# Masking the first attention rows on TensorE, one scale of x for two chunks, and a re-priced instruction order in a fused attention + MLP kernel

## The chip, the cores and the metric

The kernel runs on one core of one Trainium2 chip. Its metric is the device time of one execution in microseconds (us); the time given for a kernel is the median of its runs.

## The reference

```python
scores = (1/sqrt(64)) * q @ k.T              # 4 batches, 12 heads, 448 rows, head size 64
scores = where(causal mask, -1e9, scores)
attn = exp(scores - max(scores)); attn = attn / (sum(attn) + 1e-9)
x = (attn @ v)  -> 1792 x 768                # heads side by side
h = x @ w_in                                 # w_in 768 x 2048
out = (h - tanh(h)) @ w_out                  # w_out 2048 x 768
```

q, k, v are float32; w_in and w_out arrive as float64.

## The kernel before, in words

TensorE (PE) multiplies float16 numbers, so most operands are split into a high and a low float16 part, and each product is three matmuls (high·high, high·low, low·high). `split` (L410) makes the parts: `scaled` writes the high one, and the low one is the source times a scale minus the high one, either one `scalar_tensor_tensor` on VectorE (DVE) or a scaling in place and a subtraction, both on GpSimd (POOL). Where the result of a matmul is split (`split_x`, L568) the low part is always DVE's.

The work has these parts. `first_rows` (L595) does the first 128 rows of each batch, two batches (a chunk of 256 rows) per call, in six steps of four heads: eight float32 matmuls into two banks of `bank_s`, `softmax_part` per head (a DVE pass that adds the mask and takes the row's extreme, then an exponential on ScalarE, ACT, in place in SBUF), `inverse`, a product with the inverse on POOL, four transposes and eight matmuls with v through the one bank `bank_x`, and `split_x` with the scale `s_v` of v's bound. `w_in_chunk` (L452) loads 16 pieces of w_in, decodes float64 to float32 (`decode`: a shift, an ACT pass into PSUM and a DVE pass), finds a scale for each of eight column blocks, and splits. `w_out_half` (L469) does the like for w_out in two halves. `mlp_g` (L553) runs the first MLP product `mlp1` (L519) for 16 blocks `f` of the hidden size: 18 matmuls into one of two `bank_m` banks, tanh on ACT, a DVE pass out of PSUM, and a split into g; `h_scale` (L504) prepares the scales, per block for the two first chunks (`by_block`). `mlp2` (L535) is 48 matmuls, an evacuation and a store. `attention` (L735) does the other 320 rows of each batch, head pair by head pair: `prep` loads and splits q, k and v; `weights_unit` and `weights_last` make the split softmax weights, which a DMA transposes; `values` multiplies with v.

The order in time is not the program's. Each instruction (or group) becomes an entry in `Work` (L26). `schedule` (L159) is a list scheduler run at build time: each engine takes its ready entry of lowest `rank`, with durations from `cost` (L118), and the order that comes out is emitted, one in-order queue per engine. `either` (L107) gives an entry several engines, and the strings of `CFG` (L826) say which: "AVGA" for tag `w_in` means blocks 0, 1, 2, 3 on ACT, DVE, POOL, ACT, and so on round. `RANK` (L827) holds the ranks of the parts: before, `c0` (first chunk's rows) -14.3, `att0` -13.3, `w_in` -12.8, `evac` (what empties `bank_m`) 4.2, `w_out` 7.5, `c0b` (second chunk's rows) 9.3; the MLP's matmuls run at 10 and above and the later attentions from 8.5 up. An entry that uses the SBUF port which DVE and POOL share is marked `shared` (L96 to L102), and the planner keeps two such entries from overlapping (L182, L202).

`load_v(0)` writes into `x_block`, where `first_rows` also puts x, so attention of batch 0 comes after `mlp1` of both first chunks.

Of the kernel before, what the change touches and what calls it, by code (L numbers as in the profile page):

```python
# [20 lines left out]
P = 128  # L21
# [4 lines left out]
class Work:  # L26
# [43 lines left out]
    def add(self, eng, method, args, kw):  # L70
# [36 lines left out]
    def either(self, tag, *ways):  # L107
# [6 lines left out]
        n = self.turn[tag] = self.turn.get(tag, -1) + 1  # L114
        way = CFG[tag]
        self.ops[-1].update(eng=way[n % len(way)], tag=(tag, n))

    def cost(self, eng, method, outs, ins):  # L118
# [18 lines left out]
        if eng == "A":  # L137
            return n * 0.833 + (51 if psum else 94) + 93 * aps + 93 * (len(outs) > 1), 0.0
        if eng == "G":
            if method == "tensor_tensor":  # L140
                return n * 1.885 + 148, 0.0
# [17 lines left out]
    def schedule(self):  # L159
# [15 lines left out]
        for _ in range(n):  # L175
# [6 lines left out]
            if e in o["shared"] and port > t:  # L182
# [19 lines left out]
            if e in o["shared"]:  # L202
                t = max(t, port)
                port = t + o["cost"]
# [14 lines left out]
            for j in users[i]:  # L219
                left[j] -= 1  # L220
                f = self.ops[j]["eng"]
                at[j] = max(at[j], end + (self.SAME if f == e else self.LAT)[f])
# [36 lines left out]
def attention_then_mlp(ctx, tc, qk, v, w_in, w_out, out):  # L259
# [52 lines left out]
    ones = buf([P, P], BF16, "ones")  # L312
    mask = buf([P, 3 * P], F32, "mask")
# [31 lines left out]
    small = buf([P, 192], F32, "small")  # L345
# [25 lines left out]
    G.affine_select(out=m, in_=m, pattern=[[-1, P]], compare_op=ALU.is_ge, fill=NEG, base=0, channel_multiplier=1)  # L371
    V.memset(mask_last, 0.0)
# [47 lines left out]
    us_in, us_out, us_in_max = cols(8), cols(2), cols(1)  # L420
# [24 lines left out]
    def w_in_chunk(j):  # L445
# [9 lines left out]
        acc, s = r_acc(), r_s1()  # L455
# [38 lines left out]

    r_ch, r_usg, r_sg, r_uo, r_mix = col_ring(2, 8), col_ring(2, 1), col_ring(2, 8), col_ring(2, 2), col_ring(2, 2)

    def new_chunk(n, at=0):
# [3 lines left out]
        c.ch, c.usg, c.sg, c.uo = r_ch(), r_usg(), r_sg(), r_uo()  # L501
# [51 lines left out]
    def mlp_g(c, g16=g16, tag="g", by_block=False):  # L553
        if not by_block:
            rank(RANK["evac"])
            h_scale(c)
        for f in range(NF):
            j = f // 2
            if by_block and f % 2 == 0:
# [28 lines left out]
    r_total, r_min = col_ring(3, 4), col_ring(3, 4)  # L588
# [6 lines left out]
    def first_rows(c, bs, blocks, xs, r0):  # L595

        qkf = [view(block, at, [NP, 2, P], F32) for block, at in blocks[:2]]
        vf = view(*blocks[2], [2, NP, 2 * D], F32)
        for i, b in enumerate(bs):
# [4 lines left out]
            rank(r0)  # L604
            S.dma_start(vf[:, i], v[b, :, :, 0])
        mv, c.us_x, s_v = cols(1), cols(1), cols(1)
        bound(mv, vf.rearrange("p a n d -> p (a n d)"))
        bound_scale(c.us_x, s_v, mv, 2, mx_c)
        x = view(x_block, xs * 4 * P * NP * 2, [NP, 2, 2 * P], F16)
        c.x = [x[:, i] for i in range(NP)]  # L610
        for i in range(2):
            for g in range(H // 4):
                total, mn = r_total(), r_min()
# [244 lines left out]
```

## Time and profile before

| | |
|---|---|
| time, median of 3 runs | 605.71 us (604.11 to 606.19) |
| profiled execution, own time | 603.75 us |
| its span (first to last instruction) | 602.0 us |
| PE busy | 559.2 us (93%) |
| DVE busy | 451.6 us (75%) |
| ACT busy | 294.8 us (49%) |
| POOL busy | 312.9 us (52%) |
| DMA, mean | 123 GB/s; 327 to 337 GB/s from 15 to 45 us |

An engine's busy time is summed over its instructions. Busy shares are means over stages that have different limits, so the stages have to be read one by one. Matmuls are pipelined: what counts on PE is the distance between them, which a run of them in the timeline gives.

### The profile page before, as it was taken

What the parts mean: (1) busy time and instruction counts of PE and PEld (TensorE: products, weight loads), DVE (VectorE), ACT (ScalarE), POOL (GpSimd) and SP (SyncE); (2) the same over time, 40 slices, a digit from 0 to 9 for tenths busy, and PEclk for the clock granted to TensorE, in tenths of its full rate; (3) what the DMA queues carried; (4) which work ended last, traced back from release to release, by engine and by line L of the source; (5) the groups of instructions that cost most, each with busy time, mean ns of one, the idle gap of its engine ahead of it and who ended that gap; (6) DMA issues with size and microseconds to landing.
All of it is one profiled execution on the core that took longest, in us unless ns stands there. A gap on an engine that the chain in (4) does not pass through costs nothing.

```text
span 602.0 us, 13635 instructions
## 1 busy us (share of the span) xinstructions
PE 559.2 (93%) x5144; PEld 375.9 (62%) x5144; DVE 451.6 (75%) x1286; ACT 294.8 (49%) x796; POOL 312.9 (52%) x389
## 2 busy tenths in 40 slices
PE   3688689999999999999999999999999999999997
PEld 3456468876555556765666666665666566776664
DVE  3889997989999999999959999921999961332000
ACT  5899899983366755553436463400644430121000
POOL 3577962883232157886528788510687820465000
PEclk9999899999999999999999999999999999999999
DMA  8995467645386974448563556640334281000100
GB/s 283 327 337 186 141 196 212 188 127 222 95 164 142 181 164 79 80 99 181 119 141 72 106 123 174 128 74 27 84 60 79 42 146 43 13 2 1 27 27 26
DMA packets 113378, 74.02 MB, mean 123 GB/s; under 512 B 89760, under 2 KB 99488, under 8 KB 112800
## 3 DMA queue, kind: packets, MB, share of 16 engines
q1 hardware_dynamic: 113312, 73.15, 48.8%
q8 instruction: 40, 0.66, 0.5%
q14 instruction: 26, 0.21, 0.1%
HBM read 45.61 MB, written 5.51 MB: 85 GB/s over the span
## 4 chain that ended last, share of the span: by engine, by line
PE 31%; DVE 31%; issue 3%; DMA 3%; POOL 3%; ACT 1%; DVEq 0%; SPq 0%; POOLq 0%; ACTq 0%
PE b_m L232 29%; DVE pn L232 6%; DVE prob L232 6%; DVE small L232 5%; DVE first L232 3%; DVE t L232 3%; DVE g L232 2%; PE b_x L232 2%; DVE v L232 2%; DVE k L232 1%; DMA e<-in_v_dram 1%; DVE x L232 1%; DMA slot<-in_qk_dram 1%; POOL g L232 1%; DMA pt<-pn 1%
## 5 line engine op out<-in xcount | busy, mean ns | idle before, releaser
L232 PE MATMUL b_m<-x,w_in 128*128 128x320 f16 (+1 forms) x1728 | 230.1, 291 | 15.3 <-DVE t L232 14.2
L232 PEld LDWEIGHTS <-w_in 128*128 128x128 f16 x1728 | 167.5, 98 | 72.1 <-issue 22.9
L232 PE MATMUL b_m<-slot,g 128*128 128x384 f16 x1152 | 192.4, 326 | 0.0
L232 PEld LDWEIGHTS <-g 128*128 128x128 f16 x1152 | 110.7, 98 | 74.9 <-issue 3.9
L232 ACT ACTIVATE prob<-prob,small 128x256 f32<-128x256 f32 (+2 forms) x102 | 58.8, 577 | 70.0 <-DVE small L232 69.5
L232 POOL TENSOR_SCALAR t<-t,small 128x320 f32<-128x320 f32 (+1 forms) x80 | 53.4, 668 | 51.6 <-DVE g L232 43.9
L232 ACT ACTIVATE t<-b_m,small 128x320 f32<-128x320 f32 (+1 forms) x96 | 48.1, 502 | 63.7 <-PE b_m L232 53.6
L232 DVE SCALAR_TENSOR_TENSOR t<-b_m,small,t 128x320 f32<-128x320 f32 (+1 forms) x96 | 49.9, 520 | 30.2 <-ACT t L232 30.0
L232 DVE TENSOR_SCALAR o<-b_m,small 128x384 f32<-128x384 f32 x28 | 17.1, 610 | 70.3 <-PE b_m L232 70.2
L232 POOL TENSOR_TENSOR g<-t,g 128x320 f16<-128x320 f32 x64 | 54.2, 847 | 5.3
L232 DVE CUSTOM_DVE_ANT_0 prob<-b_s,mask,small 128x384 f32<-128x384 f32 (+1 forms) x87 | 46.1, 545 | 0.2
L232 DVE SCALAR_TENSOR_TENSOR slot<-b_s,e 128x384 int32<-128x384 int32 x64 | 34.6, 547 | 5.5 <-ACT b_s L232 3.2
L232 DVE SCALAR_TENSOR_TENSOR pn<-prob,small,pn 128x256 f16<-128x256 f32 (+2 forms) x60 | 37.5, 645 | 0.1
L232 PEld LDWEIGHTS <-v 128*64 128x64 f16 x1296 | 31.5, 111 | 8.2 <-issue 8.0
L232 PE MATMUL b_m<-slot,first 128*128 128x384 f16 x192 | 33.6, 326 | 0.0
L232 PEld LDWEIGHTS <-first 128*128 128x128 f16 (+2 forms) x282 | 21.7, 98 | 17.6 <-issue 6.2
L232 PE MATMUL b_s<-k,q 64*128 64x256 f16 (+2 forms) x342 | 30.7, 317 | 0.4 <-DVE small L232 0.3
L232 ACT ACTIVATE e<-slot 128x768 f32<-128x768 f32 (+1 forms) x30 | 26.3, 876 | 5.4 <-DMA slot<-in_moe_w_in_dram 3.5
L232 POOL TENSOR_SCALAR prob<-prob,small 128x384 f32<-128x384 f32 (+2 forms) x24 | 15.4, 640 | 24.5 <-DVE pn L232 16.3
L232 DVE TENSOR_SCALAR g<-t,small 128x320 f16<-128x320 f32 x48 | 27.1, 564 | 0.4
L232 PE MATMUL b_x<-pt,v 128*64 128x64 f16 (+1 forms) x1026 | 26.3, 207 | 0.3 <-DMA pt<-pn 0.3
L232 DVE TENSOR_SCALAR small<-small 128x1 f32<-128x1 f32 (+4 forms) x159 | 26.0, 178 | 0.2
(137 smaller groups left out, 815.9 us busy)
## 6 DMA issues: line engine op xcount, KB each, us to landing
slot<-in_moe_w_in_dram SPq DMA_DIRECT2D x16, 768.0 KB, 6.2
slot<-in_qk_dram SPq DMA_DIRECT2D x18, 384.0 KB, 3.3
slot<-in_moe_w_out_dram SPq DMA_DIRECT2D x8, 768.0 KB, 4.7
e<-in_moe_w_out_dram SPq DMA_DIRECT2D x8, 768.0 KB, 4.5
e<-in_v_dram SPq DMA_DIRECT2D x3, 1536.0 KB, 6.6
out_dram<-o SPq DMA_DIRECT2D x24, 192.0 KB, 1.9
first<-in_qk_dram SPq DMA_DIRECT2D x6, 384.0 KB, 3.4
g<-in_qk_dram SPq DMA_DIRECT2D x6, 256.0 KB, 6.5
```

The source lines that it names most:

```text
L232: getattr(self.eng[o["eng"]], method)(*args, **kw)
```

## The change

It does four things. In the first rows, two bfloat16 matmuls per step (identity times the mask, 256 columns) start the two banks, and the eight score matmuls add to them; DVE takes maxima of two heads at a time out of PSUM, one small DVE instruction turns the four maxima into biases, and the exponentials read PSUM and write SBUF. The scale of x is one for both first chunks (`first_values`), so the second chunk needs no scales of its own for h, and `h_scale` has two instructions instead of three. `split` has a third way for low parts: scaling on ACT, subtraction on POOL. The planner's prices and its rule for the shared port are altered, and every string of `CFG` and every rank of `RANK` is new.

```diff
-            two_ports = method == "tensor_scalar" and len(big) == 1 and outs[0].dtype == big[0].dtype and len(ins) == 1
+            two_ports = method == "tensor_scalar" and len(big) == 1 and not any(x.space == bass.MemoryType.PSUM for x in outs + ins)
...
-            return n * 0.833 + (51 if psum else 94) + 93 * aps + 93 * (len(outs) > 1), 0.0
+            words = ins[0].space != bass.MemoryType.PSUM and (o.space == bass.MemoryType.PSUM or ins[0].ap[-1][0] > 1)
+            return n * 0.833 + (51 if psum else 94) + 93 * aps + 93 * (len(outs) > 1) + 75 * (words and not aps), 0.0
...
-            if e in o["shared"] and port > t:
+            lead = 190.0 if e == "V" else 135.0
+            if e in o["shared"] and port - lead > t:
...
-                t = max(t, port)
-                port = t + o["cost"]
+                t = max(t, port - lead)
+                port = t + o["cost"] + (75.0 if e == "V" else 22.0)
...
     def split(hi, lo, src, s, tag):
-        def lo_pool():
-            G.tensor_scalar(src, src, s, 1.0, ALU.mult, ALU.mult)
-            G.tensor_tensor(lo, src, hi, ALU.subtract)
         scaled(hi, src, s, tag)
-        wk.either(tag + "_lo", lambda: V.scalar_tensor_tensor(lo, src, s, hi, ALU.mult, ALU.subtract), lo_pool)
+        wk.either(tag + "_lo", lambda: wk.nothing("V"), lambda: G.tensor_scalar(src, src, s, 1.0, ALU.mult, ALU.mult),
+                  lambda: A.activation(src, src, AF.Copy, scale=s))
+        wk.either(tag + "_lo", lambda: V.scalar_tensor_tensor(lo, src, s, hi, ALU.mult, ALU.subtract),
+                  lambda: G.tensor_tensor(lo, src, hi, ALU.subtract), again=True, A="G")
...
     def h_scale(c, j=slice(0, 8)):
         V.tensor_scalar(c.ch[:, j], us_in[:, j], c.us_x, None, ALU.mult)
-        V.tensor_scalar(c.sg[:, j], c.ch[:, j], 2.0 ** 15, 2.0 ** -100, ALU.mult, ALU.max)
-        V.reciprocal(c.sg[:, j], c.sg[:, j])
+        V.tensor_scalar(c.sg[:, j], s_in[:, j], c.s_h, 2.0 ** 100, ALU.mult, ALU.min)
...
+    def first_values(vs, r0):
+        for n, vf in enumerate(vs):
+            rank(r0)
+            for i in range(2):
+                S.dma_start(vf[:, i], v[2 * n + i, :, :, 0])
+            bound(mv[:, n:n + 1], vf.rearrange("p a n d -> p (a n d)"))
+        with wk.group():
+            for n in range(2):
+                over_partitions(mv[:, n:n + 1], 2 + n)
+        V.tensor_reduce(mx_c, bank_1[:, 2 * P:], axis=AX.X, op=ALU.max)
+        scales(us_x, s_v, mx_c, 1e-30)
+        V.tensor_scalar(s_h, s_v, 2.0 ** -15, None, ALU.mult)
...
                 with wk.group():
+                    for j in range(2):
+                        T.matmul(pS[j], ident16, mask16.unsqueeze(1).to_broadcast([P, 2, P]), start=True, stop=False)
                     for t in range(2):
                         for j in range(2):
                             a = qkf[i][j * D:(j + 1) * D, 2 * g + t]
-                            T.matmul(pS[j][:, t], a[:, 0], a[:, 1], start=True, stop=True)
+                            T.matmul(pS[j][:, t], a[:, 0], a[:, 1], start=False, stop=(t == 1))
+                for j in range(2):
+                    V.tensor_reduce(mx[:, 2 * j:2 * j + 2], pS[j], axis=AX.X, op=ALU.max)
+                V.tensor_scalar(nm, mx, -(D ** -0.5), None, ALU.mult)
                 for j in range(2):
                     for t in range(2):
-                        h = 2 * t + j
-                        softmax_part(e[:, h], pS[j][:, t], mask[:, 2 * P:], -(D ** -0.5), mn[:, h:h + 1], total[:, h:h + 1])
+                        h = 2 * j + t
+                        A.activation(e[:, h], pS[j][:, t], AF.Exp, bias=nm[:, h:h + 1], scale=D ** -0.5, accum_out=total[:, h:h + 1])
...
     c = new_chunk(2 * P)
-    first_rows(c, (0, 1), [(g_block, i * 8 * H * D) for i in range(3)], 0, RANK["c0"])
+    vs = [view(block, at, [2, NP, 2 * D], F32) for block, at in ((g_block, 16 * H * D), (TS[7], 0))]
+    first_values(vs, RANK["v0"])
+    first_rows(c, (0, 1), [(g_block, i * 8 * H * D) for i in range(2)], vs[0], 0, RANK["c0"])
...
-    first_rows(c2, (2, 3), [(TS[5 + i], 0) for i in range(3)], 1, RANK["c0b"])
-    mlp_g(c, tag="g0", by_block=True)
+    c2.ch, c2.sg = c.ch, c.sg
+    first_rows(c2, (2, 3), [(TS[5 + i], 0) for i in range(2)], vs[1], 1, RANK["c0b"])
+    mlp_g(c, tag="g0", scales_of="blocks")
...
-    mlp_g(c2, g2, "g2", by_block=True)
+    mlp_g(c2, g2, "g2", scales_of=None)
...
-CFG = {"early": 4, "e_bufs": 4, "b_out": "A", "b_qk": "AAV", "shift_in": "AGG", "inverse": "A", "w_in": "AVGA", "w_in_lo": "GGV", "shift_out": "AVAG", "w_out": "VAAA", "w_out_lo": "V", "p0": "G", "p0t": "AVAA", "x0": "VVVAAV", "g0": "GGGA", "g0_lo": "V", "g2": "GVVV", "g2_lo": "G", "g": "VVGV", "g_lo": "G", "o": "V", "k_first": "VAVGGA", "k_first_lo": "VVGV", "q_first": "G", "q_first_lo": "V", "v_first": "GVA", "v_first_lo": "V", "p_first": "AGGAVA", "p_first_lo": "V", "k": "GVGG", "k_lo": "V", "q": "VA", "q_lo": "G", "v": "GVAV", "v_lo": "GVV", "p": "VAVV", "p_lo": "VGV", "x": "AAVA"}
-RANK = {"c0": -14.292, "w_in": -12.778, "evac": 4.208, "w_out": 7.476, "c0b": 9.316, "att0": -13.314, "att": -0.165}
+CFG = {"early": 4, "e_bufs": 4, "b_out": "V", "b_qk": "AVA", "shift_in": "AGA", "inverse": "VAAVVV", "w_in": "G", "w_in_lo": "V", "shift_out": "AAGGVG", "w_out": "AGGA", "w_out_lo": "AVV", "p0": "G", "p0t": "AV", "x0": "AAVA", "g0": "AAAGVG", "g0_lo": "GGAGVA", "g2": "A", "g2_lo": "AVGG", "g": "VAAAAA", "g_lo": "AVAG", "o": "VVAAAA", "k_first": "GAV", "k_first_lo": "VGAG", "q_first": "A", "q_first_lo": "V", "v_first": "AV", "v_first_lo": "AVVV", "p_first": "AV", "p_first_lo": "VG", "k": "AAAV", "k_lo": "A", "q": "GAVVAG", "q_lo": "VG", "v": "VVGAAA", "v_lo": "V", "p": "AVV", "p_lo": "GGVA", "x": "VAA"}
+RANK = {"v0": -31.343, "c0": -30.647, "w_in": -12.927, "evac": -0.075, "w_out": 6.819, "c0b": -10.251, "att0": -33.946, "att": -4.124}
```

## Rows read from the trace of the kernel before

**Rows 1.** The page: the span in 40 equal slices, the busy tenths of PE and DVE.

```profile
PE   3688689999999999999999999999999999999997
DVE  3889997989999999999959999921999961332000
```

**Rows 2.** Busy time by stretches of the span. Columns: stretch, its length, busy us (instructions) of PE, of the weight loads, of DVE, ACT and POOL, then the granted clock, the DMA share and GB/s.

```profile
0.00:15.00 15.00, 5.66 (x30) 4.48 (x31) 4.85 (x33) 8.72 (x33) 5.38 (x12) 1.00 0.86 283
15.00:40.00 25.00, 17.75 (x104) 12.35 (x104) 21.37 (x85) 21.89 (x56) 17.58 (x13) 1.00 1.00 337
40.00:86.00 46.00, 35.63 (x314) 28.11 (x315) 42.70 (x168) 43.05 (x103) 35.46 (x26) 0.96 0.57 181
86.00:136.50 50.50, 47.51 (x431) 40.44 (x428) 44.81 (x99) 44.38 (x96) 31.93 (x44) 1.00 0.63 182
136.50:200.00 63.50, 62.26 (x563) 36.42 (x561) 61.96 (x166) 33.31 (x95) 16.84 (x23) 1.00 0.62 160
200.00:300.00 100.00, 97.42 (x1028) 62.96 (x1027) 99.19 (x281) 52.38 (x158) 64.94 (x86) 1.00 0.60 124
300.00:400.00 100.00, 97.73 (x1025) 64.09 (x1024) 84.21 (x231) 44.59 (x133) 64.52 (x83) 1.00 0.60 125
400.00:503.60 103.60, 100.45 (x1039) 65.53 (x1037) 73.71 (x195) 37.57 (x110) 52.92 (x70) 1.00 0.35 68
503.60:602.00 98.40, 94.82 (x632) 61.50 (x630) 18.87 (x37) 8.88 (x17) 23.36 (x36) 0.99 0.05 17
```

**Rows 3.** The timeline of PE, merged: start, us, instruction, count, and in brackets the idle time before it and what ended it.

```profile
3.83 1.23 PE L232 MATMUL b_s<-g 64*128 64x128 f32 x8 [3.83 <-DMA g<-in_qk_dram]
...
24.18 1.09 PE L232 MATMUL b_x<-ident,pn 128*128 128x128 f32 x4 [3.21 <-DVE small L232]
...
35.75 1.44 PE L232 MATMUL b_scales<-w_in,ones 128*128 128x256 bf16 x6
...
40.45 0.82 PE L232 MATMUL b_m<-x,w_in 128*128 128x256 f16 x6
41.10 0.82 PE L232 MATMUL b_scales<-w_in,ones 128*128 128x256 bf16 x6
...
70.85 1.99 PE L232 MATMUL b_m<-x,w_in 128*128 128x256 f16 x12 [2.53 <-DVE t L232]
...
94.35 0.63 PE L232 MATMUL b_x<-ident,pn 128*128 128x128 f32 x4
...
136.49 13.81 PE L232 MATMUL b_m<-slot,g 128*128 128x384 f16 x84
```

**Rows 4.** What PE waited for, from 0 to 110 us (first row) and from 136.5 us on (second row): us in total, times, longest.

```profile
PE b_m L232 <- DVE t L232: 7.7, 6, 2.5
...
PE b_m L232 <- DVE t L232: 4.7, 8, 1.0
```

**Rows 5.** The last piece of the chain that ended last: start, us, engine and what it writes, instructions.

```profile
503.62 94.82 PE b_m L232 x630
```

**Rows 6.** Groups of DVE instructions by shape, whole span: output<-inputs, shapes, count, busy us, mean ns of one, idle time before.

```profile
L232 DVE CUSTOM_DVE_ANT_0 pn<-b_s,mask 128x128 f32<-128x128 f32 x48 | 11.6, 282 | 4.9 <-PE b_s L232 4.8
L232 DVE DVE_READ_ACCUMULATOR2_ANT small<- 128x1 f32 x168 | 13.3, 79 | 0.0
L232 DVE TENSOR_REDUCE small<-b_scales 128x1 f32<-128x256 f32 x8 | 3.3, 416 | 1.2 <-PE b_scales L232 1.2
L232 DVE TENSOR_REDUCE small<-g 128x1 f32<-128x1536 f32 x1 | 1.8, 1754 | 0.0
L232 DVE TENSOR_SCALAR small<-small 128x1 f32<-128x1 f32 x78 | 12.5, 173 | 0.1
L232 DVE SCALAR_TENSOR_TENSOR w_in<-slot,small,w_in 128x1536 f16<-128x1536 f32 x2 | 3.9, 1954 | 0.3 <-POOL w_in L232 0.3
L232 DVE SCALAR_TENSOR_TENSOR slot<-slot,small,slot 128x768 f16<-128x768 f32 x16 | 17.3, 1095 | 0.1
L232 DVE SCALAR_TENSOR_TENSOR g<-t,small,g 128x256 f16<-128x256 f32 x16 | 9.7, 623 | 0.8 <-ACT g L232 0.6 <-POOL g L232 0.2
L232 DVE TENSOR_SCALAR g<-t,small 128x320 f16<-128x320 f32 x48 | 27.1, 564 | 0.4
L232 DVE TENSOR_SCALAR o<-b_m,small 128x384 f32<-128x384 f32 x28 | 17.1, 610 | 70.3 <-PE b_m L232 70.2
L232 DVE SCALAR_TENSOR_TENSOR k<-slot,small,k 128x448 f16<-128x448 f32 x14 | 12.0, 857 | 0.0
L232 DVE SCALAR_TENSOR_TENSOR pn<-prob,small,pn 128x384 f16<-128x384 f32 x24 | 16.2, 695 | 0.0
L232 DVE SCALAR_TENSOR_TENSOR pn<-prob,small,pn 128x256 f16<-128x256 f32 x24 | 11.8, 513 | 0.0
```

**Rows 7.** The same for ACT.

```profile
L232 ACT ACTIVATE pn<-pn,small 128x128 f32<-128x128 f32 x48 | 18.7, 393 | 3.6 <-DVE small L232 3.5
L232 ACT ACTIVATE t<-b_m,small 128x256 f32<-128x256 f32 x32 | 14.8, 467 | 2.5 <-PE b_m L232 2.0 <-POOL first L232 0.4
L232 ACT ACTIVATE e<-slot 128x768 f32<-128x768 f32 x16 | 13.5, 843 | 1.6 <-DVE slot L232 1.6
L232 ACT ACTIVATE first<-slot,small 128x320 f16<-128x320 f32 x3 | 1.7, 562 | 6.6 <-DVE small L232 6.6
L232 ACT ACTIVATION_READ_ACCUMULATOR pn<-pn,small 128x1 f32 x48 | 9.2, 192 | 0.0
```

More of the change, by code (lines that the diff above doesn't have):

```diff
@@ L105, in add, with either @@
         op["move"] += move
-    def either(self, tag, *ways):
+    def either(self, tag, *ways, again=False, A="A"):
         self.ops.append(dict(alts={}, deps=set(), rank=self.rank, move=0.0))
@@ L113, in either, with nothing @@
         self.alt = None
-        n = self.turn[tag] = self.turn.get(tag, -1) + 1
-        way = CFG[tag]
-        self.ops[-1].update(eng=way[n % len(way)], tag=(tag, n))
+        n = self.turn[tag] = self.turn.get(tag, -1) + (not again)
+        way = CFG[tag].replace("A", A)
+        self.ops[-1].update(eng=way[n % len(way)], tag=(tag, n), A=A)
+    def nothing(self, eng):
+        self.ops[-1]["alts"][eng] = [], [0.0]
+        self.ops[-1].setdefault("shared", set())
     def cost(self, eng, method, outs, ins):
@@ L221, in schedule @@
                 f = self.ops[j]["eng"]
-                at[j] = max(at[j], end + (self.SAME if f == e else self.LAT)[f])
+                at[j] = max(at[j], end + (self.LAT[f] if f != e else self.SAME[f] if o["cost"] else 0.0))
                 if not left[j]:
@@ L312, in attention_then_mlp @@
     ones = buf([P, P], BF16, "ones")
+    mask16 = buf([P, P], BF16, "mask16")
     mask = buf([P, 3 * P], F32, "mask")
@@ L344, in attention_then_mlp @@
     v16_ring = Ring([view(v16_block, i * 16 * P, [2, 4, 2 * D], F16) for i in range(4)])
-    small = buf([P, 192], F32, "small")
+    small = buf([P, 208], F32, "small")
     used = [0]
@@ L371, in attention_then_mlp @@
     G.affine_select(out=m, in_=m, pattern=[[-1, P]], compare_op=ALU.is_ge, fill=NEG, base=0, channel_multiplier=1)
+    V.tensor_copy(mask16, m)
     V.memset(mask_last, 0.0)
@@ L453, in w_in_chunk @@
             decode(y[:, a * 3:(a + 1) * 3], t, scratch(i), "_in")
-        acc, s = r_acc(), r_s1()
+        acc, s = r_acc(), s_in[:, j:j + 1]
         mag = w_in16[j][:, 0].bitcast(BF16)
@@ L492, in w_out_half @@
                 split(w_out16[n][m][:, 0, part], w_out16[n][m][:, 1, part], ys[m][:, part], s_out[n][:, 2 * m + a:2 * m + a + 1], "w_out")
+    r_sh = col_ring(2, 1)
     r_ch, r_usg, r_sg, r_uo, r_mix = col_ring(2, 8), col_ring(2, 1), col_ring(2, 8), col_ring(2, 2), col_ring(2, 2)
@@ L500, in new_chunk @@
         c.n, c.at, c.x, c.rank = n, at, [], 10.0
-        c.ch, c.usg, c.sg, c.uo = r_ch(), r_usg(), r_sg(), r_uo()
+        c.ch, c.usg, c.sg, c.uo, c.s_h = r_ch(), r_usg(), r_sg(), r_uo(), r_sh()
         return c
@@ L551, in mlp2, with mlp_g @@
             S.dma_start(out[dst:dst + r1 - r0, n * HALF:(n + 1) * HALF], o[r0:r1, :])
-    def mlp_g(c, g16=g16, tag="g", by_block=False):
-        if not by_block:
+    def mlp_g(c, g16=g16, tag="g", scales_of="all"):
+        if scales_of == "all":
             rank(RANK["evac"])
@@ L558, in mlp_g @@
             j = f // 2
-            if by_block and f % 2 == 0:
+            if scales_of == "blocks" and f % 2 == 0:
                 rank(RANK["evac"])
@@ L585, in inverse @@
         V.reciprocal(total, total)
-    r_total, r_min = col_ring(3, 4), col_ring(3, 4)
+    r_total, r_max, r_min = col_ring(3, 4), col_ring(2, 4), col_ring(3, 4)
     e4_ring = Ring([view(pn_block, n * 16 * P, [4, P], F32) for n in range(3)])
@@ L593, in evacuated, with first_rows @@
         wk.either(tag, lambda: A.activation(o, i, AF.Copy), lambda: V.tensor_copy(o, i))
-    def first_rows(c, bs, blocks, xs, r0):
-        qkf = [view(block, at, [NP, 2, P], F32) for block, at in blocks[:2]]
-        vf = view(*blocks[2], [2, NP, 2 * D], F32)
+    us_x, s_v, s_h, mv = cols(1), cols(1), cols(1), cols(2)
+    def first_values(vs, r0):
[10 more added lines that the diff above has]
+        V.tensor_scalar(s_h, s_v, 2.0 ** -15, None, ALU.mult)
+    def first_rows(c, bs, blocks, vf, xs, r0):
+        qkf = [view(block, at, [NP, 2, P], F32) for block, at in blocks]
+        c.us_x, c.s_h = us_x, s_h
         for i, b in enumerate(bs):
@@ L603, in first_rows @@
                 S.dma_start(qkf[i][:, pairs].rearrange("p n x t -> p n (x t)"), qk[b, pairs, :, 0:2 * P].rearrange("n p t -> p n t"))
[L604 to L608, printed above, removed]
         x = view(x_block, xs * 4 * P * NP * 2, [NP, 2, 2 * P], F16)
@@ L612, in first_rows @@
             for g in range(H // 4):
-                total, mn = r_total(), r_min()
+                total, mx, nm = r_total(), r_max(), r_min()
                 e = e4_ring()
@@ L637, in first_rows @@
                         for j in range(2):
-                            T.matmul(px[64 * j:64 * j + 64, t], vf[:, i, 2 * g + t, j * D:(j + 1) * D], pt[:, 2 * t + j], start=True, stop=True)
+                            T.matmul(px[64 * j:64 * j + 64, t], vf[:, i, 2 * g + t, j * D:(j + 1) * D], pt[:, 2 * j + t], start=True, stop=True)
                 split_x(x[:, 2 * g:2 * g + 2, :, i * P:(i + 1) * P], px, "x0", s_v)
@@ L740, in attention @@
         bound_scale(c.us_x, sv, m1, 3, mx_v)
+        V.tensor_scalar(c.s_h, sv, 2.0 ** -15, None, ALU.mult)
         def at(hp):
```

4 lines of the change are left out of this document (2 added, 2 removed).

## The prediction

> **What bounds the kernel now.** I read the slices first [rows 1]: PE is at nine tenths from about 85 us on, and DVE from 15 to about 300 us. Then the stretches [rows 2], which split the span in three. From 0 to 136.5 us (*start*: first rows, w_in, half of w_out, the first MLP product of two chunks) PE is busy 5.66 + 17.75 + 35.63 + 47.51 = 106.6 us, so idle 29.9, of which 26.9 lie before 86 us. From 136.5 to 503.6 (*middle*: the two chunks' second product and the four attentions with their MLP) PE is busy 357.9 of 367.1 us, idle 9.2. The *end* is one run of 630 matmuls in 94.82 us, 150 ns each [rows 5]; nothing of the change shortens that. So at most some 39 us can be had from idle PE, three quarters of it before 86 us.
>
> The timeline of PE shows the start [rows 3]: first matmul at 3.83 us, when q and k land; second group of transposes only at 24.18, behind DVE; first MLP matmul at 40.45; last transposes of the second chunk at 94.35; second product from 136.49. From 15 to 86 us DVE is busy 64.1 of 71 us, ACT 64.9, POOL 53.0 [rows 2]: PE starves because DVE and ACT are full. In the middle DVE is full too, 61.96 of 63.5 and 99.19 of 100 us up to 300 us, while ACT is at half; yet PE's waits for DVE's emptying of its banks are short, 7.7 us up to 110 and 4.7 us after 136.5 [rows 4].
>
> **The change part by part.** *Masks on PE.* Twelve steps with two matmuls of 256 columns: 24. The nearest rows are six of the same size in 1.44 us at 35.75 and in 0.82 us at 41.10 [rows 3], 0.24 and 0.137 us each (the same shape takes nearly twice as long early, although the granted clock reads 1.00 in both stretches [rows 2]). Twelve at either: 4.5 us more for PE, all before 100 us, beside PE's idle 26.9. I take 0 on the path; uncovered it is 4.5.
>
> *Maxima and exponentials.* 48 passes of 282 ns go, 13.5 us, each with an accumulator read of 79 ns behind it, 3.8 if these add in full and 0 if they lie within the passes. In come 24 reductions of 128x256 from PSUM at 416 ns, 10.0, and 12 small ones at 173, 2.1 [rows 6]. DVE gains 1.4 to 5.2; I take 4. The 48 exponentials took 393 ns from SBUF; no row shows 128 columns from PSUM with a pointer; ACT took 467 for 256 columns from PSUM [rows 7], 128 columns fewer at most 467 and not under half of it, 234. I take 360: -1.6 us on ACT, bounds -7.6 to +3.6.
>
> *A bank held longer.* Before, a score bank is free after DVE's pass; now after reduction, bias and exponentials: per step 2 x 0.416 + 0.173 + 4 x 0.36 = 2.4 us on two engines in turn, plus PE's 1.2, some 4 us with handoffs. The second transposes came 14 us after the first in the profile because one `bank_x` bank waits for v's scale; the twelve steps end at 94.35 [rows 3], 7.5 us a step. So 4 us is covered as long as ACT serves these steps promptly; if not, see the third rival.
>
> *One scale of x.* 2 chunks x 8 blocks x 3 small DVE instructions become 16: 32 fewer at 173 ns [rows 6], -5.5 us of DVE. SP's queue: v of the second chunk (two loads of 384 KB) moves ahead of q and k of batch 1, 0.79 MB at 337 GB/s [rows 2], 2.3 us later for these; the `bank_x` chain stands still till 24 us then anyway, so nothing, or 2.3. x's first split now waits for both chunks' bounds, one more reduction of 1.75 us (the 1754 ns row [rows 6]) in DVE's queue; all of DVE's work behind it shifts by that, but it is only moved.
>
> *New engines, start.* Counted from the strings, DVE: `b_out` 16 reductions of 768 elements, estimated at 0.86 between the 416 and 1754 ns rows: +13.8; `w_in_lo` 6 x 1.954: +11.7; `w_out_lo` 6 x 1.095: -6.6; `g0_lo` 14 x 0.623: -8.7; `g2` 12 at 0.47: -5.6; the others (`w_in`, `w_out`, shifts, `p0t`, `x0`, `g2_lo`, `inverse`) about -2. Sum +2.6, with the first rows and the scales 2.6 - 4 - 5.5 = **-7 us** of 113.7. ACT: `b_out` leaves (16 x 0.843 and a read of 0.192 each [rows 7], -16.6), g, shifts and low parts come; about -6 of 118.0. POOL: `w_in_lo` -28, low parts of g and w_out and `w_in` +27: unchanged.
>
> *New engines, middle.* DVE: `g` 37 x 0.564 = -20.9; `p_lo` 38 at 0.65 (between 695 and 513) = -24.7; `k_lo` 18 x 0.857 = -15.4; `o` 18 x 0.610 = -11.0; `p_first_lo` 15 x 0.65 = -9.8; against `g_lo` 16 x 0.65 = +10.4 and `inverse`, `v_lo`, `q_lo`, `p_first` about +22; smaller ones -10. Sum **-59 us** of DVE's 338 after 136.5. ACT takes +94 (of it `g` 53 x 0.55, 29; low parts 43), from 177 to 271 of 465; POOL -3.
>
> Does ACT do a moved pass as fast as DVE? DVE's high part of g, 320 columns, took 564 ns, ACT 562 for 320 columns from SBUF with a scale [rows 6, 7]: equal, so the load moves one for one. The Trainium skill ("ScalarE: Activation LUTs", Rules for kernel authors) speaks against such a move: multiplications belong on VectorE, which it puts at up to about 3 times ScalarE's rate in bf16. No row here shows that for float32 in and float16 out; were it so, moving the 37 passes of g would free DVE of 7 us and not 21 (an estimate from that page), and the gain in the middle would be nearer its lower bound.
>
> **The sum.** Start: DVE and ACT set its rate, and both lose some 6 of about 115 us; that shortens the stretch before 86 us by 6 if the order is as good as before. The second chunk's rows, `c0b`, now stand ahead of the emptying of `bank_m`: both chunks' MLP work is then ready per block of w_in, which can fill more of the idle 26.9. Bounds: -20 (idle before 86 down to some 7) and +12 (third rival). I take -6, nearest the engines' loads. Middle: with DVE from 87% to about 71% of its time, half of the 9.2 idle goes: -4; bounds -9 and, if ACT's longer queue delays tanh, +10. End: 0. Sum -10: 603.75 - 10 = 593.75 for the profiled execution; the median of the runs shown is 1.96 above it, so 595.7.
>
> **The rivals.** *The start packs much better* (22%): with both chunks' first product ready early, PE's idle before 86 us falls by 16 rather than 6, and the middle gives 4: 585.7. For it: each block of w_in then holds 72 matmuls, 9.9 us at the 0.137 of the six at 40.45 [rows 3], instead of 4.9. Against: the DMAs and DVE's and ACT's 90% are as before.
>
> *Relief off the path* (10%): PE is dense from 86 us; what DVE saves in the middle turns into DVE idle time, and the start keeps its length since the 26 us that move onto DVE there (`b_out`, `w_in_lo`) sit on w_in's path. Gain 0 to 3: about 604.5. For it: the waits of PE are only 4.7 us in the middle [rows 4].
>
> *First rows crowd out the emptying of `bank_m`* (18%): slower. Each of the second chunk's six steps holds ACT for 4 x (0.36 + a read of 0.192 [rows 7]), 2.2 us, and its share of `p0t` and `x0` besides, about 3 us, ranked ahead of tanh. If they come while the first chunk's MLP runs, the two banks stay full: 6 x 3 = 18 us of PE standing, as in the 2.53 us wait at 70.85 [rows 3], of which the denser run later gives back half. Net +9 in the start; the 4 in the middle are then eaten by ACT's queue: 605.7 + 9 = 614.7, down to about 608 if fewer steps collide. It decides once a tanh waits longer than the 18 matmuls of one `f`, 2.5 us, beyond the other bank. Against: the planner knows ranks and both banks.
>
> **How the numbers follow.** Forecast 50%, rivals 22, 10 and 18. A measurement of this kernel tells about 0.3%, 1.8 us, from no change. Faster: 50 + 22 and some of the second rival, 0.74; same 0.08; slower 0.18. The range takes in the first rival with 2 to spare and of the third its near half: 583.5 to 608. The forecast's own range is 590 to 601.
>
> **What would show it.** Second product beginning at about 130 us instead of 136.5; DVE busy near 385 us, ACT near 380, POOL near 310; DVE no longer at 99% from 200 to 300 us; PE idle in the middle about 5 us; the last run of matmuls unchanged at 150 ns each. Wrong would be: PE waiting in `b_m` for DVE or ACT for more than 15 us, the first MLP matmul much after 45 us, or score matmuls waiting for ACT.

## The result, and the profile after

The changed kernel took 613.0 us (median of 4 runs, 611.5 to 614.7) where the kernel before took 605.4 in the same session: ratio 1.0134, 95% interval 1.0106 to 1.0162. It is slower by 7.6 us; the prediction said 595.7, with 583.5 to 608 as its range. The profiled execution took 613.81 us for a span of 612.1. That is 10.1 us more than the span of before's profile, because before's profiled execution (603.75 us) lies 1.6 below its median and this one 0.8 above.

The first part of the page of the changed kernel, busy us of each engine (share of the span) and instructions, then the busy tenths in 40 slices of the span:

```profile
PE 569.8 (93%) x5168; PEld 378.7 (62%) x5168; DVE 419.6 (69%) x1126; ACT 371.1 (61%) x922; POOL 300.4 (49%) x368
...
PE   3578889899999999999999999999999999999997
...
DVE  3798899998899999999989999998012310232000
```

PE's row begins 3578889 where it was 3688689 [rows 1]. DVE did lose load, 32 us of 451.6, but the row shows where: it is as full as before up to 390 us, fuller up to 428, and stands at 0 to 3 from there on, where before had nines from 421 to 482 [rows 1]. The windows show where the time is. Columns as in [rows 2]; the second product begins at 144.76 us, so the last two rows are the whole start and all that follows:

```profile
0.00:15.00 15.00, 5.26 (x28) 3.45 (x30) 5.55 (x19) 8.12 (x25) 3.48 (x10) 1.00 0.83 271
15.00:40.00 25.00, 16.16 (x92) 10.35 (x88) 20.49 (x58) 18.59 (x48) 9.37 (x9) 1.00 1.04 343
40.00:86.00 46.00, 38.71 (x307) 29.92 (x306) 41.38 (x104) 38.45 (x97) 26.67 (x24) 0.96 0.54 170
86.00:144.80 58.80, 53.87 (x475) 45.52 (x473) 54.59 (x113) 47.41 (x109) 40.03 (x53) 0.97 0.61 177
...
0.00:144.80 144.80, 113.99 (x893) 89.23 (x894) 122.00 (x291) 112.57 (x276) 79.55 (x94) 0.98 0.69 213
144.80:612.10 467.30, 455.81 (x4278) 289.46 (x4275) 297.56 (x836) 258.53 (x646) 220.85 (x275) 1.00 0.44 92
```

The same two stretches of the kernel before:

```profile
0.00:136.50 136.50, 106.56 (x869) 85.38 (x870) 113.72 (x382) 118.04 (x285) 90.34 (x93) 0.99 0.70 221
136.50:602.00 465.50, 452.68 (x4278) 290.50 (x4275) 337.93 (x905) 176.73 (x511) 222.58 (x297) 1.00 0.43 94
```

So 8.3 of the 10.1 us of longer span are lost in the start and 1.8 behind it, although DVE has 40 us less to do there and PE the same 4278 instructions. PE's timeline has the first loss early (start, us, instruction, count, idle before and what ended it):

```profile
8.20 0.37 PE L239 MATMUL b_s<-mask,ident 128*128 128x256 bf16 x1 [3.23 <-ACT pn L239]
...
10.54 1.12 PE L239 MATMUL b_x<-ident,pn 128*128 128x128 f32 x4
...
21.79 0.37 PE L239 MATMUL b_s<-mask,ident 128*128 128x256 bf16 x1 [3.00 <-ACT pn L239]
...
29.68 1.08 PE L239 MATMUL b_x<-ident,pn 128*128 128x128 f32 x4
...
49.37 1.49 PE L239 MATMUL b_m<-x,w_in 128*128 128x256 f16 x6
```

The second group of transposes comes at 29.68 instead of 24.18 us, the first MLP matmul at 49.37 instead of 40.45 [rows 3]. Score matmuls now wait for ACT (`pn`, the exponentials), which they never did before. In the waits of PE from 0 to 144.8 us (us in total, times, longest) that line is new, the first one was 0.3 us before, and the wait for DVE's emptying of `bank_m` has fallen (9.4 us up to 136.5 before):

```profile
PE b_scales L239 <- ACT w_in L239: 8.4, 4, 4.0
PE b_s L239 <- ACT pn L239: 7.9, 6, 3.2
PE b_m L239 <- DVE t L239: 6.6, 7, 2.3
```

DVE and ACT at the third step (its score matmuls start at 16.16 us) show how the wait of 3.00 us at 21.79 arises:

```profile
17.42 0.76 DVE L239 TENSOR_REDUCE small<-b_s 128x2 f32<-128x256 f32 x2 [2.39 <-PE b_s L239]
19.00 1.75 DVE L239 TENSOR_REDUCE small<-g 128x1 f32<-128x1536 f32 x1 [0.82 <-DMA g<-in_v_dram]
20.68 0.16 DVE L239 TENSOR_SCALAR small<-small 128x4 f32<-128x4 f32 x1
...
21.66 1.75 DVE L239 TENSOR_REDUCE small<-slot 128x1 f32<-128x1536 f32 x1 [0.50 <-DMA slot<-in_v_dram]
```

```profile
20.93 0.37 ACT L239 ACTIVATE pn<-b_s,small 128x128 f32<-128x128 f32 x1 [2.39 <-DVE small L239]
...
26.76 1.48 ACT L239 ACTIVATE w_in<-slot 128x1536 bf16<-128x1536 f32 x1 [0.42 <-DVE slot L239]
28.15 0.46 ACT L239 ACTIVATE x<-b_x,small 128x256 f16<-128x256 f32 x1
```

The maxima are there at 18.2, the biases only at 20.8: the small instruction stands in DVE's queue behind the reduction of v, which itself waited 0.82 us for its DMA. The four exponentials follow, and the fourth step's scores enter the first bank only behind two of them (21.79), the second behind all four. Meanwhile the second v is reduced (21.66 to 23.4). x's first split, which needs both bounds, comes at 28.15 instead of 23.03, on ACT and behind a pass over w_in.

### The profile page after: what moved, and what is told of

Its sections match the earlier page's. It is cut to its first block, busy times and chain, and to the rows that moved or that the text cites. A ratio compares the mean times of both kernels' runs of the same rounds, so it can differ in the third digit from the quotient of the medians.

```text
span 612.1 us, 13686 instructions
## 1 busy us (share of the span) xinstructions
PE 569.8 (93%) x5168; PEld 378.7 (62%) x5168; DVE 419.6 (69%) x1126; ACT 371.1 (61%) x922; POOL 300.4 (49%) x368
## 4 chain that ended last, share of the span: by engine, by line
PE 43%; DVE 28%; DMA 11%; issue 7%; ACT 5%; POOL 5%; SPq 2%; DVEq 0%; POOLq 0%; ACTq 0%
PE b_m L239 38%; DVE small L239 7%; DVE prob L239 5%; DMA slot<-in_moe_w_in_dram 4%; DVE pn L239 4%; DMA e<-in_v_dram 3%; DVE first L239 2%; PE b_x L239 2%; DVE slot L239 2%; DVE v L239 2%; DVE t L239 2%; DMA slot<-in_moe_w_out_dram 2%; DVE x L239 2%; SPq L239 2%; PE b_s L239 1%
## 5 line engine op out<-in xcount | busy, mean ns | idle before, releaser
L239 POOL TENSOR_TENSOR g<-t,g 128x320 f16<-128x320 f32 (+1 forms) x62 | 51.3, 829 | 120.8 <-ACT t L239 116.3
L239 ACT ACTIVATE prob<-prob,small 128x384 f32<-128x384 f32 (+2 forms) x120 | 67.8, 572 | 25.5 <-DVE small L239 19.8
L239 ACT ACTIVATE o<-b_m,small 128x384 f32<-128x384 f32 x18 | 10.3, 571 | 94.9 <-PE b_m L239 94.9
L239 DVE TENSOR_SCALAR small<-small 128x2 f32<-128x2 f32 (+5 forms) x207 | 46.0, 238 | 26.9 <-ACT o L239 22.7
L239 ACT ACTIVATE t<-b_m,small 128x320 f32<-128x320 f32 (+1 forms) x96 | 47.9, 501 | 23.1 <-PE b_m L239 20.8
L239 POOL TENSOR_SCALAR prob<-prob,small 128x384 f32<-128x384 f32 (+2 forms) x51 | 33.3, 656 | 34.6 <-DVE pn L239 16.6
L239 ACT ACTIVATE g<-t,small 128x320 f16<-128x320 f32 (+1 forms) x62 | 34.0, 551 | 24.5 <-DVE t L239 24.2
L239 DVE CUSTOM_DVE_ANT_0 prob<-b_s,mask,small 128x256 f32<-128x256 f32 (+1 forms) x87 | 46.5, 547 | 1.2 <-POOL pn L239 0.7
L239 POOL TENSOR_TENSOR pn<-prob,pn 128x256 f16<-128x256 f32 (+2 forms) x47 | 41.4, 887 | 5.9 <-ACT prob L239 4.6
L239 DVE TENSOR_SCALAR o<-b_m,small 128x384 f32<-128x384 f32 x10 | 6.1, 613 | 41.6 <-PE b_m L239 41.6
L239 POOL TENSOR_SCALAR t<-t,small 128x256 f32<-128x256 f32 (+1 forms) x33 | 19.6, 596 | 22.1 <-ACT g L239 18.5
L239 ACT ACTIVATE t<-t,small 128x320 f32<-128x320 f32 (+1 forms) x41 | 22.3, 545 | 10.0 <-DVE g L239 7.6
```

The lines of the kernel that those rows point to most:

```text
L239: getattr(self.eng[o["eng"]], method)(*args, **kw)
```

## The experiments

The times are medians, the ratios are to the kernel before on the same chip; "second product" is its first matmul in the profiled execution, "rest" the span from there on.

**One part undone, the order made again.** Four kernels change one thing in the changed kernel and let `schedule` order the rest anew.

e1, the strings (`CFG`) and ranks of before:

```diff
...
-RANK = {"v0": -31.343, "c0": -30.647, "w_in": -12.927, "evac": -0.075, "w_out": 6.819, "c0b": -10.251, "att0": -33.946, "att": -4.124}
+RANK = {"v0": -14.293, "c0": -14.292, "w_in": -12.778, "evac": 4.208, "w_out": 7.476, "c0b": 9.316, "att0": -13.314, "att": -0.165}
```


> The changed kernel with CFG and RANK of the kernel before (v0 ranked with c0, -14.29); masks on PE, exponentials from PSUM, one scale and the new prices stay. Theory C (the new strings and ranks cost the 8 us): 604 to 607, second product from about 137 us. Theory F (banks held until the exponentials have read them) or S (first x waits for the second chunk's v): 610 to 616, second product from 142 us or later.

649.4 us, ratio 1.071 (1.067 to 1.075); second product at 179.20. The new softmax with the old strings is by far the worst order: the second chunk's last transposes start at 138.84 us (94.35 before [rows 3]), and from 86 to 136.5 us PE is busy for 28.3 of 50.5 us, with a granted clock that reads 0.70.

e2, the softmax by way of SBUF:

```diff
-                for j in range(2):
-                    V.tensor_reduce(mx[:, 2 * j:2 * j + 2], pS[j], axis=AX.X, op=ALU.max)
-                V.tensor_scalar(nm, mx, -(D ** -0.5), None, ALU.mult)
...
+                        softmax_part(e[:, h], pS[j][:, t], mask[:, 2 * P:], -(D ** -0.5), nm[:, h:h + 1], total[:, h:h + 1])
```


> The changed kernel with the softmax of the first rows as before (mask and maximum by one DVE pass per head, exponential in place in SBUF, no mask matmuls); one scale, prices, strings and ranks stay new. Theory F: 604 to 607, first MLP matmul at about 42 us. Theory C or S: 611 to 615, first MLP matmul still at 47 us or later.

624.6 us, ratio 1.030 (1.027 to 1.033).

e3, a scale of x for each chunk:

```diff
...
-                split_x(x[:, 2 * g:2 * g + 2, :, i * P:(i + 1) * P], px, "x0", s_v)
+                split_x(x[:, 2 * g:2 * g + 2, :, i * P:(i + 1) * P], px, "x0", c.s_v)
```


> The changed kernel with a scale of x for each chunk again (the second chunk's v loaded and reduced with its rows; 24 small DVE instructions more). Theory S: second group of transposes at about 24 us and not 29.7, first MLP matmul near 43 us, time 605 to 608. Theory C or F: second transposes may come earlier but the time stays within 611 to 615.

621.1 us, ratio 1.024 (1.020 to 1.028). The second transposes come back to 24.20, the first MLP matmul to 45.86, but the second product begins at 145.30 all the same, and the rest is 474.7 us (467.3 in the changed kernel).

e4, the old prices of `cost` and of the shared port:

```diff
...
-            lead = 190.0 if e == "V" else 135.0
+            lead = 0.0
...
```


> The changed kernel with the planner's prices and port rule as before (no lead, no trailing time, ACT and POOL prices as before, float16 results of one-input DVE passes not counted on the port). If the prices are what lengthens the start: 604 to 608. If not: 611 to 617, as the strings were not made for these prices.

621.4 us, ratio 1.025 (1.022 to 1.028). All four are slower than the changed kernel itself and lie outside every range expected of them. An order made again differs in more than the altered part, as e3's longer rest shows, so such runs can't price a part. The next ones keep an order as it is and edit only what is emitted.

**The softmax in the order of before.** Three steps toward the change, with before's order kept. e9 only adds the masks on PE (DVE's pass adds zeros):

```diff
...
+                mm["calls"] = [("matmul", (pS[j], ident16, mask16.unsqueeze(1).to_broadcast([P, 2, P])), dict(start=True, stop=False)) for j in range(2)]
...
-                        softmax_part(e[:, h], pS[j][:, t], mask[:, 2 * P:], -(D ** -0.5), mn[:, h:h + 1], total[:, h:h + 1])
+                        softmax_part(e[:, h], pS[j][:, t], mask[:, :P], -(D ** -0.5), mn[:, h:h + 1], total[:, h:h + 1])
```


> The kernel before, its planned order kept, with the mask added by two matmuls per step and nothing else (DVE's pass adds zeros, writes SBUF as before, exponentials in SBUF). If PE's 24 more matmuls are a part of what lengthens the start: 608 or more. If they are covered by idle PE, as predicted: 604 to 607.

605.9 us, ratio 1.001 (0.999 to 1.003): the 24 matmuls cost nothing that can be measured. e10 adds to it that the exponentials read PSUM, so that the banks are held; DVE's passes stay:

```diff
...
+                        wk.ops[-1]["calls"] = [("activation", (e[:, h], pS[j][:, t], AF.Exp), dict(bias=mn[:, h:h + 1], scale=D ** -0.5, accum_out=total[:, h:h + 1]))]
```


> As the kernel with the masks on PE in the order of before, and the exponentials read PSUM too (DVE's four passes stay, so no DVE time is saved; exponentials stand at their old places, or right ahead of the next step's matmuls). Only the time for which a step holds its two banks differs from the kernel with the masks alone. Theory F (holding the banks costs): 615 to 630, PE waits of score matmuls for ACT near 20 us. If the waits of the full softmax came from its reductions instead: 605 to 609.

614.7 us, just under theory F's range, ratio 1.016 (1.013 to 1.019), second product at 148.00. Its waits of PE up to 136 us, and the rest of its span:

```profile
PE b_s L245 <- ACT pn L245: 13.6, 12, 2.8
```

```profile
148.00:614.00 466.00, 453.13 (x4278) 290.29 (x4275) 339.39 (x908) 176.97 (x511) 221.07 (x297) 1.00 0.43 94
```

Holding the banks costs 9 us, all of it ahead of the second product. The hold could not be had quite alone: nine of the 48 exponentials had to move ahead of two or three other ACT instructions, so as to stand before the next step's matmuls. e5 is the whole new softmax, with two reductions and the one small instruction, in the same order:

```diff
...
+                wk.ops[-2]["calls"] = [("tensor_reduce", (mx[:, 2 * a:2 * a + 2], pS[a]), dict(axis=AX.X, op=ALU.max)) for a in range(2)]
+                wk.ops[-2]["calls"] += [("tensor_scalar", (mn, mx, -(D ** -0.5), None, ALU.mult), {})]
```


> The kernel before, its planned order kept on every engine, with the new softmax of the first rows put into it (masks on PE, two maxima and one small instruction at the place of the fourth DVE pass, exponentials from PSUM at their old places, or right ahead of the next step's matmuls where they stood later); two scales, old strings, old prices. Theory F (the new softmax holds the two score banks until the exponentials, and that lengthens the start in any order): 610 to 618, second product from 142 us or later. Theory C (strings and order cost the 8 us, the new softmax is about free): 602 to 607.

627.5 us, ratio 1.037 (1.034 to 1.041), second product at 160.30, the rest 464.9. The same wait is now longer:

```profile
PE b_s L234 <- ACT pn L234: 22.2, 14, 3.2
```

It is over the 610 to 618 expected. In e10 the first exponential can start when the first head's pass is done; here all four wait for both reductions and the biases, which stand at the place of the fourth pass. That is the main difference between the two runs, and they lie 13 us apart.

**Parts undone in the order of the changed kernel.** e6 puts the softmax by way of SBUF back:

```diff
...
+                    wk.ops[-1]["late"] = k, [("tensor_tensor_reduce", (e[:, 2 * j + t], pS[j][:, t], mask[:, 2 * P:]), dict(op0=ALU.add, op1=ALU.min, scale=-(D ** -0.5),
+                                              scalar=3.4e38, accum_out=nm[:, 2 * j + t:2 * j + t + 1])) for t in range(2)]
...
+                        wk.ops[-1]["calls"] = [("activation", (e[:, h], e[:, h], AF.Exp), dict(bias=nm[:, h:h + 1], scale=-1.0, accum_out=total[:, h:h + 1]))]
```


> The changed kernel, its planned order kept on every engine, with the old softmax of the first rows put back at the same places (two DVE passes per head pair where the reduction stood, exponentials in place in SBUF, no masks on PE). Theory F: 604 to 608, no waits of score matmuls for exponentials, second product from about 138 us. Theory C or S: 611 to 615 (gains at most the 1.3 us of the table load).

612.0 us, ratio 1.012 (1.010 to 1.014); second product at 141.70, rest 468.7. No score matmul waits for an exponential any more, but the time is what theories C and S said, not F: in this order the new softmax costs 3 us of the start and about 1 us of the time. The changed kernel itself stood at 1.013 (1.011 to 1.016) and was not run again beside e6, e7, e11 and e12; its interval overlaps all of theirs, so small differences among them are not sure. e7 leaves the second chunk's bound out of the scale of x (that v is not reduced):

```diff
...
+            if n == 1:
+                wk.ops[-1]["mark"] = "drop"
...
```


> The changed kernel, its planned order kept, with the scale of x taken from the first chunk's v alone: the reduction of the second chunk's v and its product are left out. Theory S (the first x waits for the second v): second transposes at 27 us or before (now 29.7), time 608 to 611. Other theories: time 612 to 614, since x's split stands behind the same work in ACT's queue.

610.7 us, ratio 1.009 (1.006 to 1.012); second product at 138.90, rest 469.3. The time is theory S's, but x's first split comes only 1.0 us earlier (27.13) and the second transposes at 28.58, not at 27. e11 does both, with the edits of e6 and e7 together:

> The changed kernel, its planned order kept, with both undone at once: softmax of the first rows in SBUF without masks, and the scale from the first chunk's v alone. If the two waits are what this order has lost: 603 to 607. If the order itself is the slower one: 609 to 612, start shorter than 140 us but the rest longer than the 465.5 us of before.

612.7 us, ratio 1.012 (1.008 to 1.016), close to what was expected if the order itself is the slower one. Its profiled execution was the fastest of four, and even that shows a start of 139.4 and a longer rest:

```profile
0.00:139.40 139.40, 103.71 (x868) 84.28 (x869) 119.35 (x350) 113.39 (x276) 79.86 (x94) 0.95 0.71 222
139.40:607.70 468.30, 455.96 (x4278) 289.34 (x4275) 297.17 (x836) 258.52 (x646) 220.95 (x275) 1.00 0.43 92
```

With both new waits gone the kernel stays some 7 us above before: that much belongs to what is left of the change, which is above all the new order and its engines. The longest of PE's waits in that start is one that the changed kernel has too (8.4 us) and before has hardly (0.3 us), so it came with the order and not with the softmax or the scale:

```profile
PE b_scales L243 <- ACT w_in L243: 9.6, 4, 4.0
```

e12 tests a small suspicion. In the changed kernel ACT's table load waits for the first biases:

```profile
6.05 1.28 ACT L239 ACT_TABLE_LOAD   x1 [6.05 <-DVE small L239]
7.34 0.37 ACT L239 ACTIVATE pn<-b_s,small 128x128 f32<-128x128 f32 x1
```

Here a small exponential ahead of it lets it load at 0.80 us:

```diff
...
+            if early and o["eng"] == "V":
+                self.nc.scalar.activation(self.first, o["alts"]["V"][0][0][1][0][:, 0:1], AF.Exp)
...
```


> The changed kernel, its planned order kept, with one small ACT instruction at the start that waits for DVE's first memset alone, so that the load of the activation table stands at about 1 us and not behind the first maxima at 6 us. If the table load's 1.28 us lies on the chain of the first steps: first exponential at 6.1 us (now 7.34), time 611.5 to 612.5. If the chain waits for v's scale anyway: 612.5 to 613.5.

612.9 us, ratio 1.013 (1.009 to 1.017): the first exponential comes 1.3 us earlier and no gain can be measured. e8 moves six of the eight low parts of w_in from DVE back to POOL:

```diff
+            if o.get("tag", ("", 0))[0] == "w_in_lo" and o["tag"][1] % 3 < 2:
+                eng = "G"
```


> The changed kernel, its planned order kept, with the low part of w_in made on POOL for six of the eight blocks, as before (two POOL passes, 1.55 + 3.1 us, where one DVE pass of 1.96 stood). If DVE's 1.96 us in front of x's low parts are what spaces the first chunk's steps at 6 us instead of 5: transposes of the first chunk end before 52 us (now 54.4) and the time is 609 to 612. If the longer way of the block (4.7 against 2.0 us) weighs more: 613 to 618.

625.8 us, ratio 1.034 (1.032 to 1.036), second product at 155.91, slower than either range expected: in this order the low parts are not what DVE should lose.

**DVE's relief alone.** The rest is 465.5, 465.8, 466.0 and 464.9 us in the four profiles with before's order and 467.3 to 469.3 in six with the new one, where DVE has 40 us less. Either relief buys nothing there or the new order loses it. e13 takes before's order and moves only 48 passes of `g` from DVE to ACT; e14 also 28 of `o` (the line is e14's, e13 has `== "g"` in it):

```diff
...
+            eng = "A" if o.get("tag", ("", 0))[0] in ("g", "o") and o["eng"] == "V" else o["eng"]
```


> The kernel before with its order of instructions kept; only the 48 passes that scale g on DVE (564 ns each, 27 us) go to ACT in the same places. First theory, that TensorE bounds the middle and DVE's relief there buys nothing: DVE busy behind the second product's start falls from 338 to about 311 us, the length of that stretch stays at 465.5 within 1.5 us, the time within 0.3% of before (605.6). Second theory, that relief of DVE shortens the middle and the changed kernel loses it again only through its order: the stretch falls by 2 to 4 us, the time to about 602. Third, that the added ACT passes delay the tanh: the stretch grows by 2 us or more, as it did in the changed kernel (467.3).

> As the run with g on ACT, and besides it the 28 passes on DVE that empty the second product's bank into o (610 ns, 17 us) go to ACT, so DVE is relieved by 44 us in all, a little more than by the whole change in that stretch (40). First theory (TensorE bounds the middle): DVE near 294 us behind the second product's start, length still 465.5 within 2 us, time within 0.5% of before. Second theory (relief shortens it): 2 to 5 us less than before. Third (ACT in order delays what TensorE waits for): 2 to 4 us more, with TensorE busy over 455 as in the changed kernel.

e13 took 601.7 us, ratio 0.993 (0.991 to 0.995), e14 602.2, ratio 0.995 (0.992 to 0.997). Both are faster than before, by less than 1%, and faster than the changed kernel. e13's profile is of the slowest of its five executions (604.1 us, its start 139.0 us), e14's of its fastest (601.1). The rest of e13, then of e14:

```profile
138.97:602.38 463.41, 452.14 (x4278) 290.49 (x4275) 320.28 (x857) 199.10 (x559) 220.98 (x297) 1.00 0.43 95
```

```profile
136.83:599.19 462.36, 451.57 (x4278) 290.25 (x4275) 306.75 (x829) 213.22 (x587) 220.90 (x297) 1.00 0.43 95
```

With 18 and 31 us less on DVE the rest shortens by 2.1 and 3.1 us, as the second theory of each said, where the four profiles above differ by 1.1. Relief is worth something there, but little of it arrives, with PE busy for 452 of 463 us. e13's moved passes all lie behind 231 us, so the other 2 us of its 4 in the time can't come from the start by this edit; one profile of each kernel doesn't show where they lie.

e15 is the kernel before ordered again under the new prices, with the shorter working of h's scale and little else (the loads of v get entries of their own, the heads of a step another order):

```diff
...
-                port = t + o["cost"]
+                port = t + o["cost"] + (75.0 if e == "V" else 22.0)
...
```


> The kernel before (its strings and ranks, softmax by way of SBUF, two scales of x) ordered again under the new prices, with the shorter working of the scale of h. Theory one, that strings and prices belong together and each alone upsets the order: 615 to 630, as with the other orders made again under one altered part (621 to 649). Theory two, that the new prices describe the chip better and by themselves help: 600 to 605. If it is theory one, the loss shows in the start, the second product beginning after 142 us.

624.4 us, ratio 1.029 (1.025 to 1.033), second product at 148.48: the new prices don't help the old strings. The loss is not in the start alone: the rest is 474.7 us, 9 more than before, with the same engines and DVE busy for 338 us as before (PE for 456.6, granted clock 0.99). So a new order can lose time behind the second product too, with the engines unchanged.

## Why the prediction was wrong

**Masks on PE: right.** 0 on the path; e9 measured +0.3 us, within its interval. A pair took 0.58 to 0.64 us early and 0.38 later, where 0.48 and 0.27 were taken. One reading beside it was wrong: the quicker six matmuls, at 41.10, lie in a stretch whose granted clock reads 0.96, not 1.00 [rows 2]; no term hangs on it.

**Durations: right in the main, and beside the point.** An exponential out of PSUM took 368 ns (taken: 360), a pair of maxima 414 (416), a low part of w_in 1964 (1954), a reduction for `b_out` 944 (860), the bias instruction 160 to 170 at the first three steps (173).

**"-6 in the start if the order is as good as before": the step that failed.** The order was not as good. The start was sized by the engines' loads, -7 us of DVE; it grew by 8.3 us in the profile, and DVE had 122.0 us in it, +8.3 where -7 was forecast. With the softmax and the scale both undone, the new order and its engines are still 7 us slower than before's (e11, 612.7 us; 4.5 to 10 by its interval): about all of the 7.6 us measured. In the order of before, the new softmax would give 627; the new order wins back 14 of these 22 us, but brings its own loss. By e6, e7 and e11 the parts don't add: their starts are 3 to 6 us shorter than the changed kernel's and their rests 1 to 2 us longer.

**"A bank held longer ... 4 us is covered": failed too.** It set 4 us against the mean distance of 7.5 us between steps. But the mean holds waits for other engines and the steps pass through queues that are in order, so the 4 us did not fit into a gap. In the order of before they lengthened the start: +9 us in time with the hold (e10), +22 with the reductions and the bias in front of the exponentials (e5). In the new order, which was planned with the new softmax, undoing it gains only about 1 us (e6): there the hold explains little of the time. The third rival had the size (614.7) and the sign, and that is luck: its place was the emptying of `bank_m`, and PE's waits there fell from 9.4 to 6.6 us. Two of the signs that would prove the forecast wrong did come, score matmuls waiting for ACT (7.9 us) and the first MLP matmul well after 45 us (49.37). The first rival's packing did not come: work ready early doesn't help where the first rows come late.

**"Only moved": failed, by a small amount.** The second v's reduction stands in DVE's queue in front of the scale that x's first split needs, and that split moved from 23.03 to 28.15 us. The reduction is only a part of this: without it the split comes at 27.13 and the time is 2.3 us shorter (e7), with intervals that overlap, and e11 shows no gain.

**Middle, "-4 ... half of the 9.2 idle": relief helps there, but not in the new order.** In before's order 18 to 31 us less on DVE give 2 to 3 us in the stretch behind the second product and about 4 in the time (e13, e14). In the changed kernel that stretch grew by 1.8. PE's idle fell from 12.8 to 11.5 us there, and its busy time rose by 3.1 for the same instructions, spread over the groups (score matmuls of 384 columns 12.4 to 13.5 us, those with w_in 162.0 to 163.0, at mean ns within 1%). The merged timeline of that stretch has 231 pieces instead of 208, so PE changes more often between kinds of matmul; that this is the cause was not tried, and e15's longer rest has 203. The size of the relief was off as well: DVE fell by 32 us in all where the steps summed to 66; 17 of the difference are in the last section, the others were not traced.

**The end, 0: right.** The last 630 matmuls took 94.9 us in both profiles.

**Moved passes take as long on ACT: right in the mean only.** `g` took 559 ns on ACT against DVE's mean of 564 before. The second row is DVE's in the kernel before, with the shortest, the median and the longest pass:

```profile
L239 ACT ACTIVATE g<-t,small 128x320 f16<-128x320 f32 x53 | 29.6, 559 | 23.5 <-DVE t L239 23.2
...
L232 DVE TENSOR_SCALAR g<-t,small x48: 371/427/1005, 231.2 to 552.9; 128x320 f16<-128x320 f32 x48
```

So the mean of 564 that the prediction took for DVE's price mixes two kinds: the 19 passes during which no POOL pass ran took 381 ns in the mean, the 28 that had one beside them for more than half of their time 694. The rule of the Trainium skill that spoke against the move ("ScalarE: Activation LUTs", Rules for kernel authors) has the right direction for the first kind, 381 against 559. The move gains all the same (e13): behind the second product ACT was busy for 177 us of 465 and DVE for 338.

**Open.** Why the new order, with both waits undone, loses 3 us in the start and 3 behind it in the profiled execution was not settled. In the start the wait for ACT's passes over w_in is a candidate, and it was not tried. e15 and e4 show that prices, strings and structure stand together, not which of them is at fault.

## What to carry to other kernels

Freeing a PSUM bank quickly can be worth more than saving the copy that frees it, 9 us in the order of before: before letting a second engine read the bank, follow one step through every in-order queue it passes, and take the gap from the row that precedes it, not from the mean distance of steps. A sum over the engines' loads holds only for a given order. A change that needs a new order should be compared with its parts inside the old order; here one moved group of passes in the old order (601.7 us) beat the whole rewrite (613.0). Undoing a part and ordering again prices the order, not the part. And a mean over passes can mix two prices: look at the shortest and the longest before moving them.

## What was not expected of the hardware

Many of DVE's passes without a PSUM operand took longer in the new order. Rows by shape of the changed kernel (columns as in [rows 6]):

```profile
L239 DVE TENSOR_SCALAR small<-small 128x2 f32<-128x2 f32 x68 | 17.7, 269 | 23.7 <-ACT o L239 22.7 <-ACT first L239 0.5 <-ACT prob L239 0.2
...
L239 DVE SCALAR_TENSOR_TENSOR slot<-slot,small,slot 128x768 f16<-128x768 f32 x10 | 13.5, 1361 | 0.9 <-ACT slot L239 0.9
```

The first took 193 ns before (x30), the second 1095 [rows 6]. Over all groups that both kernels have, the passes from SBUF, reductions aside, took about 17 us more than at before's means (199 us), those that read PSUM 0.3 more (of 184) and reductions 0.3 (of 38). With before's strings it is about 4 us (e9) and, in the new structure, 3 (e1), so it comes with the new engines; in e13 27 us of passes left DVE and its busy time fell by 17, as the other passes from SBUF took 6 more.

The traces show what divides quick passes from slow ones: whether a POOL pass ran at the same time. Of the 68 passes over two columns in the changed kernel, the 30 with no POOL pass beside them took 162 ns in the mean, the 34 with one for more than half of their time 375. One over eight columns took 0.70 us at 112.06, while POOL ran a pass of 0.89 from 111.85. The passes of DVE out of `bank_m` with 320 columns took 547 ns alone and 540 beside POOL, and reciprocals of two columns 156 and 158, so neither cares. Before is no different in kind (two columns 165 and 257 ns); there 9 of 30 such passes ran beside POOL, here 34 of 68. The Trainium skill ("GPSIMD Engine Reference", 1. Specifications) says that GpSimd shares its SBUF interfaces with VectorE and contends with instructions that read two SBUF inputs or run in a two-port mode; the split by kind of pass agrees. No run moved POOL's passes alone.
